# Second buffers for the loads of q and the split parts of k, later and earlier units for the loads of q, k and v, a shared ring of four tiles for five, and measured times in the scheduler of an attention and feed-forward kernel

## The chip, the core and the metric

The kernel runs on one core of a Trainium2 chip. The core has five engines that run their own instruction lists in order and wait for each other by semaphores: TensorE (PE in the profile, with weight loads as PEld), VectorE (DVE), ScalarE (ACT), GpSimd (POOL) and SyncE (SP). SP issues all DMAs of this kernel. The metric is the device time of one execution in microseconds, and shorter is better.

## What is computed

Attention over 8 batches of 8 heads with 1152 positions of 64 elements, where neighbouring pairs of queries are averaged first (576 queries a head), and then a feed-forward layer with the gate h * cos(h):

```python
def _attn_ref(q, k, v) -> np.ndarray:
    B, H, S, D = q.shape
    factor = 2
    scale = 1.0 / np.sqrt(D)
    q_pool = q.reshape(B, H, S // factor, factor, D).mean(axis=3)
    scores = scale * np.matmul(q_pool, k.transpose(0, 1, 3, 2))
    scores = scores - np.max(scores, axis=-1, keepdims=True)
    attn = np.exp(scores)
    attn = attn / (np.sum(attn, axis=-1, keepdims=True) + 1e-09)
    return np.matmul(attn, v).astype(np.float32)
...
def _moe_ref(x, w_in, w_out) -> np.ndarray:
    h = x @ w_in
    g = h * np.cos(h)
    return (g @ w_out).astype(np.float32)
```

All inputs are float32: q, k and v of 8 x 8 x 1152 x 64, `w_in` of 512 x 2048 and `w_out` of 2048 x 512. The 8 x 576 rows of the attention's result, with the heads side by side, are the 4608 rows of the feed-forward layer.

## The kernel before, in words

**Pairs and units.** The heads are taken two at a time: 32 pairs, four to a batch. A pair `p` has ten units. Unit 0 holds the 64 queries a head that are left over from 512, and units 1 to 9 hold one block of 128 keys each, for 512 queries of both heads. A unit is a matrix product of scores into the PSUM tile `st` (L860, or L880 for the leftover), the exponential on ACT (L901 or L906), and the product with v into `ava` and `avb` (L927), which is written one unit later.

**Split numbers.** Products are made in fp16 with each float32 operand split into a high part and a rest. For pairs 0 to 5 (`NDIR = 6`) the exponentials stay in float32 and L927 multiplies in float32. From pair 6 on the exponential is split: ACT copies the high part (L909), and POOL (L915) or, for every third unit, DVE (L911) subtracts it for the rest.

**Preparing q, k and v of a later pair.** Each pair needs, ahead of its units:

- k in two portions, J0 (four blocks) and J1 (five blocks): `load_k` (L556) into the tile `kld`, `prep_k` (ACT L584 makes the high part, POOL L585 the rest, both into `kst`), `transpose_k` (L630, a DMA transpose into `k1`), and `copy_k` (L637, DMAs into `k2`).
- q: `load_q` (four DMAs, two at L566 and two at L573, into `qld`), `pool_q` (POOL L591 adds neighbouring queries, in place in `qld`), `prep_q1` (ACT L602, from pair 6 on DVE L604: the high part into `q1s`), `transpose_q1` (L609), `prep_q2` (POOL L617 and L623: the rest from `qld` and `q1s` into `qs2`), and `transpose_q2` (L744). The last reader of a `qld` tile is `prep_q2`, so a `qld` buffer is free again after L623.
- row maxima of the scores: `mains`, `mx_rest` and others (PE L655, L673, L695, L712 into the PSUM tile `mx`, DVE L665, L683, L705, L722 reduce them), and `m_write` puts them into `qs2`.
- v: `load_v` (L750 into `vld`), `v_max_begin` (DVE L757, then L390 writes 128 single elements to the DRAM tile `row`, and L392 reads them back to all partitions as `am`), `v_max_end`, `prep_v` and `prep_v_lo`.

The table `JOBS` says in which unit of which pair each step of pair n is written: `(-2, 1, pool_q)` stands for unit 1 of pair n-2. `kld`, `kst`, `qld` and `vld` have one buffer each.

**The feed-forward stream.** `ffn1` (PE L1174, ACT L1198 and L1201, DVE L1202) and `ffn2` (PE L1234, DVE L1250) work on chunks of 256 rows; `ew_group` takes the cosine on ACT (L1110), multiplies on DVE (L1116) and splits the gate on ACT and POOL (L1127, L1128). A chunk can start when the four pairs of its batch are done and `w_in` is prepared, and `ffn2` when `w_out` is. While units are written, a credit of `FRATE` a unit sets how much of this stream is written between them; what is left after the last unit follows at the end. `weight_steps` (loads at L442, DVE L453 to L463, PE L471, ACT L493 and L494, POOL L495) prepares the weights; `SRATE` is how many of its steps are written in a unit, first until `w_in` is ready, then after. Raw weights, the float32 copies of `w_out`'s parts, and the tiles `hsc` and `y` of `ffn1` share one ring of `NBIG` tiles (`big_take`, `big_free`).

**What sets the order.** The program as written is not the order that runs. `arrange` takes all instructions, gives each a cost, and goes through time: of the instructions whose inputs are ready by its own clock, each engine takes the one that was written first. The five lists that come out are fixed with dependencies, and each engine then runs its list in order. The costs are formulas in `estimate` and `transfer`; PE's and SP's stand in `arrange` itself (lines 140 to 152). An instruction that waits on the chip holds up everything behind it in its engine's list.

Of the kernel before, what the change touches and what calls it, by code (L numbers as in the profile page):

```python
# [19 lines left out]
P = 128  # L20
# [7 lines left out]
NBIG = 5  # L28
# [12 lines left out]
SRATE = (1.0, 0.6)  # L41
# [8 lines left out]
    "vam": 4, "es": 1, "pps": 1, "amx": 4,  # L50
# [74 lines left out]
def arrange(tc, nc, extra):  # L125
# [3 lines left out]
    for i in rec:  # L129
        rd, wr = boxes(i)  # L130
        eng = str(i.engine).split(".")[-1]
        if eng == "PE":
# [9 lines left out]
            if rd[0][4] == 4:  # L142
                c = max(n_out(wr) * 0.00167 + 0.0025, 0.112)
# [4 lines left out]
        else:  # L148
            nd = dict(eng=eng, ins=[], rd=[], wr=[], cost=0.0, lock=False)
            nodes.append(nd)  # L150
            if eng == "SP":
                nd["cost"] = 0.06
                nd["dma"], nd["lat"] = transfer(type(i).__name__, rd[0], wr[0])
            else:
                nd["cost"], nd["lock"] = estimate(i, type(i).__name__, rd, wr)
                nd["func"] = str(getattr(i, "func", "")) if eng == "Activation" else ""
# [153 lines left out]
def tile_attention_ffn(  # L310
# [241 lines left out]
    def load_k(n, js):  # L552
        b, hp = divmod(n, HP)
        nj = js.stop - js.start
        kt = sb1.tile([P, 2, KT - RB, D], F32, tag="kld", name="kld")
        nc.sync.dma_start(  # L556
            kt[:, :, 0:nj],
            k[b, 2 * hp : 2 * hp + 2].rearrange("h (p j) d -> p h j d", p=P)[:, :, js],
        )
        kld[n] = kt[:, :, 0:nj]  # L560

    def load_q(n):
        b, hp = divmod(n, HP)
        qt = sb1.tile([P, NSL, 2, D], F32, tag="qld", name="qld")
# [14 lines left out]
    def prep_k(n, js):  # L579
        kv = kld[n].rearrange("p h j d -> p j h d")  # L580
        nj = js.stop - js.start
        ks = sb1.tile([P, KT - RB, 4, D], F16, tag="kst", name="kst")[:, 0:nj]
        hi = ks[:, :, 0::3, :]
        nc.scalar.copy(hi, kv)  # L584
        nc.gpsimd.tensor_sub(ks[:, :, 1:3, :], kv, hi)  # L585
        kst[n] = ks
# [42 lines left out]
    def transpose_k(n, js):  # L629
        nc.sync.dma_start_transpose(  # L630
            k1[n % 3][:, js].rearrange("p j h c -> p (j h) c"),
            kst.pop(n).rearrange("p j a d -> p (j a d)"),
# [168 lines left out]
    def mains(c, ts):  # L801
# [7 lines left out]
        (-2, 0, lambda n: load_k(n, J0)),  # L809
        (-2, 0, load_q),  # L810
# [3 lines left out]
        (-2, 2, lambda n: load_k(n, J1)),  # L814
# [9 lines left out]
        (-2, 7, prep_q2),  # L824
        (-2, 8, mains(1, (0,))),
        (-2, 8, load_v),
        (-2, 9, mains(1, (1,))),
        (-1, 0, lambda n: copy_k(n, J1)),
        (-1, 0, mains(1, (2,))),
        (-1, 0, v_max_begin),  # L830
# [6 lines left out]
        (-1, 4, v_max_end),  # L837
        (-1, 5, prep_v),
        (-1, 6, lambda n: prep_v_lo(n, (0,))),
        (-1, 7, lambda n: prep_v_lo(n, (1,))),  # L840
# [534 lines left out]
    for n in (0, 1):  # L1375
        for dp, di, fn in JOBS:
            if dp + n < 0:
                fn(n)
# [64 lines left out]
```

## Time and profile before

| what | value |
|---|---|
| median of 3 runs | 1691.94 us (1689.31 to 1700.04) |
| the profiled execution, its own time | 1687.24 us |
| its span, first to last instruction | 1685.5 us |
| mean granted TensorE clock | 0.971 |
| ACT busy | 1199.7 us (71%) |
| DVE busy | 1154.0 us (68%) |
| POOL busy | 877.0 us (52%) |
| DMA traffic | 147.28 MB, mean 87 GB/s |

The table is read from the left of the time: the span is the stretch that the profile explains, and the 1.7 us between it and the execution's own time lie around it. A share of busy time is a mean over stages that differ: at first there are only attention and weights, then attention and feed-forward together, and at the end the feed-forward stream alone. In a timeline row of the profile, the two numbers ahead of the engine are the start and the duration, and the bracket at the end is the idle time of that engine before the row, with what ended it.

### The profile page before, as it was taken

How to read it: one execution, taken by the hardware profiler on the slowest of the kernel's cores; microseconds unless marked ns; L12 is line 12 of the kernel's file. 1: busy time of each engine (PE TensorE's matmuls, PEld its weight loads, DVE VectorE, ACT ScalarE, POOL GpSimd, SP SyncE). 2: the span in 40 equal slices, each digit the busy share in tenths (PEclk: the TensorE clock that was granted, in tenths of full speed). 3: DMA queues.
4: the chain of work that ended last, by engine and by line, in shares of the span. 5: the costliest groups of instructions: out<-in, count | busy, mean ns of one | idle time of the engine just before them, and what ended most of it. 6: DMA issues, size and time to landing. Idle time of an engine off the chain costs nothing. (4 is left out here: it accounts for less than half of the span.)

```text
span 1685.5 us, 39430 instructions
## 1 busy us (share of the span) xinstructions
PE 1552.6 (92%) x16580; PEld 1058.8 (63%) x16580; DVE 1154.0 (68%) x1625; ACT 1199.7 (71%) x1468; POOL 877.0 (52%) x738
## 2 busy tenths in 40 slices
PE   2889799998999989988899999999999999998998
PEld 1667677765766566655666566666666657665664
DVE  6687878688767768866667676777768778642442
ACT  2465657788977777876787687987788878885542
POOL 3242334376465746556466465564757484653222
PEclk9799999999999999998999999999999999998999
DMA  9985852455336442434325424444434443011010
GB/s 206 197 187 130 181 128 34 90 83 129 54 78 108 83 88 56 108 61 96 72 64 99 90 57 91 89 71 96 105 70 88 94 86 80 17 35 26 13 32 19
DMA packets 340657, 147.28 MB, mean 87 GB/s; under 512 B 247808, under 2 KB 323584, under 8 KB 340480
## 3 DMA queue, kind: packets, MB, share of 16 engines
q1 hardware_dynamic: 340480, 144.78, 41.1%
q8 instruction: 129, 2.11, 0.6%
q14 instruction: 48, 0.39, 0.2%
HBM read 76.55 MB, written 10.50 MB: 52 GB/s over the span
## 5 line engine op out<-in xcount | busy, mean ns | idle before, releaser
L915 POOL TENSOR_TENSOR pp<-e,pp 128x512 f16<-128x512 f32 x348 | 424.9, 1243 | 289.6 <-ACT pp L909 182.6
L665 DVE TENSOR_REDUCE mxs<-mx 128x2 f32<-128x1024 f32 x252 | 307.7, 1221 | 135.7 <-PE mx L655 132.4
L1174 PE MATMUL f<-xT,w 128*128 128x256 f16 x3168 | 385.4, 276 | 10.5 <-DVE y L1202 6.4
L1174 PEld LDWEIGHTS <-w 128*128 128x128 f16 x3456 | 339.4, 99 | 84.3 <-issue 14.4
L906 ACT ACTIVATE e<-st,eb 128x1024 f32<-128x1024 f32 x260 | 288.8, 1111 | 139.6 <-PE st L860 113.4
L1234 PE MATMUL f<-w,g 128*128 128x512 f16 x1584 | 369.0, 382 | 0.0
L1234 PEld LDWEIGHTS <-g 128*128 128x128 f16 x1728 | 167.3, 99 | 193.7 <-issue 7.1
L909 ACT CAST pp<-e 128x1024 f16<-128x1024 f32 x260 | 271.4, 1044 | 10.9 <-PE ava L927 3.6
L927 PEld LDWEIGHTS <-pp 128*128 128x128 f16 (+1 forms) x6864 | 229.5, 100 | 66.8 <-POOL pp L915 19.0
L1128 POOL TENSOR_TENSOR g<-hsc,g 128x512 f16<-128x512 f32 x144 | 197.8, 1398 | 137.0 <-ACT g L1127 136.8
L927 PE MATMUL ava<-vc,pp 128*128 128x65 f16 (+4 forms) x4680 | 254.6, 205 | 13.7 <-POOL pp L915 11.4
L860 PE MATMUL st<-q1T,k 128*128 128x512 f16 x576 | 223.2, 388 | 21.0 <-ACT e L906 12.3
L860 PE MATMUL st<-q2T,k 128*128 128x512 f16 x576 | 223.6, 388 | 0.0
L927 PE MATMUL avb<-vc,pp 128*128 128x65 f16 (+2 forms) x3240 | 213.5, 205 | 5.5 <-POOL pp L915 5.5
L655 PE MATMUL mx<-k,q1T 128*128 128x512 f16 x504 | 154.3, 389 | 25.4 <-DVE mxs L665 14.4
L860 PEld LDWEIGHTS <-k 128*128 128x128 f16 x1152 | 104.1, 100 | 116.3 <-issue 32.4
L1116 DVE TENSOR_TENSOR hsc<-hsc,y 128x512 f32<-128x512 f32 x144 | 132.3, 964 | 36.2 <-ACT y L1110 35.9
L585 POOL TENSOR_TENSOR kst<-kld,kst 128x512 f16<-128x512 f32 x64 | 89.3, 1395 | 124.8 <-ACT kst L584 111.9
L1202 DVE SCALAR_TENSOR_TENSOR y<-f,r1a,y 128x512 f32<-128x512 f32 x132 | 98.2, 746 | 79.4 <-ACT y L1201 78.9
L911 DVE TENSOR_TENSOR pp<-e,pp 128x1024 f16<-128x1024 f32 x86 | 123.7, 1439 | 28.7 <-ACT pp L909 27.6
L1198 ACT ACTIVATE hsc<-f,r 128x512 f32<-128x512 f32 x132 | 90.0, 683 | 58.9 <-PE f L1174 58.3
L901 ACT ACTIVATE pp<-st,eb 128x1024 f32<-128x1024 f32 x60 | 66.7, 1112 | 79.1 <-PE st L860 66.0
(134 smaller groups left out, 1754.5 us busy)
## 6 DMA issues: line engine op xcount, KB each, us to landing
vld<-in_v_dram SPq DMA_DIRECT2D x32, 576.0 KB, 4.0
qld<-in_q_dram SPq DMA_DIRECT2D x64, 256.0 KB, 3.9
kld<-in_k_dram SPq DMA_DIRECT2D x32, 320.0 KB, 3.3
kld<-in_k_dram SPq DMA_DIRECT2D x32, 256.0 KB, 3.9
wraw<-in_moe_w_in_dram SPq DMA_DIRECT2D x8, 1024.0 KB, 7.4
wraw<-in_moe_w_out_dram SPq DMA_DIRECT2D x8, 1024.0 KB, 6.7
out_dram<-ob SPq DMA_DIRECT2D x32, 256.0 KB, 2.5
k<-k SPq DMA_DIRECT2D x64, 80.0 KB, 2.8
```

The lines of the kernel that those rows point to most:

```text
L655: nc.tensor.matmul(m[:, h, :], q1T[n][:, 2 * t + h, :], k1[n % 3][:, c * RB : (c + 1) * RB, h, :], start=True, stop=True, skip_group_check ...
L665: nc.vector.reduce_max(mxs[n][:, 2 * t : 2 * t + 2, c], m, axis=AX.X)
L860: nc.tensor.matmul(s[:, h, :].rearrange("p (t c) -> p t c", c=P), w[:, j, h, :], x[:, h : 2 * QT : 2, :], start=part == 0, stop=part == 1, ...
L906: nc.scalar.activation(e, s, AF.Exp, scale=exp_scale, bias=eb)
L909: nc.scalar.copy(pp[:, 0], e)
L911: nc.vector.tensor_sub(pp[:, 1], e, pp[:, 0])
L915: nc.gpsimd.tensor_sub(pp[:, 1, c], e[:, c], pp[:, 0, c])
L927: mm = nc.tensor.matmul(out, w, x, start=start, stop=False, skip_group_check=True)
L1116: nc.vector.tensor_mul(hj, hj, y[:, j : j + 2])
L1128: nc.gpsimd.tensor_sub(gt[:, 1], hj, gt[:, 0])
L1174: mm = nc.tensor.matmul(ps[:, fi, :], w1[wt][:, hp, fs], ck.xT[hp][:, xi, cs], start=n == 0, stop=n == 3 * HP - 1, skip_group_check=True,)
L1234: nc.tensor.matmul(po, gt[:, gi, f % 2, ts_], w2[wt][:, f, :], start=f == 0 and (gi, wt) == (0, 0), stop=f == NF - 1 and (gi, wt) == (1, 0),)
```

## The change

It has these parts:

- `qld` and `kst` get two buffers each, and `kld` and `kst` are remembered by pair and portion, so that two of them can be under way.
- `load_k` of J0 and `load_q` move from unit 0 of pair n-2 to units 5 and 6 of pair n-3. `load_k` of J1 moves from unit 2 to unit 1. `prep_q2` moves from unit 7 to unit 9, `load_v` from unit 8 of pair n-2 to unit 0 of pair n-1, and the steps on v behind it by one unit each. The steps written ahead of the first unit now include pair 2.
- `NBIG` goes from 5 to 4, and the first value of `SRATE` from 1.0 to 0.7.
- In `arrange`, the cost of a float32 matmul is doubled, and that of an SP instruction goes from 0.06 to 1.35 for a transpose and 0.55 for another DMA.

```diff
-NBIG = 5
+NBIG = 4
...
-SRATE = (1.0, 0.6)
+SRATE = (0.7, 0.6)
...
-    "vam": 4, "es": 1, "pps": 1, "amx": 4,
+    "vam": 4, "qld": 2, "kst": 2, "es": 1, "pps": 1, "amx": 4,
...
             if rd[0][4] == 4:
-                c = max(n_out(wr) * 0.00167 + 0.0025, 0.112)
+                c = 2 * max(n_out(wr) * 0.00167 + 0.0025, 0.112)
...
             if eng == "SP":
-                nd["cost"] = 0.06
+                nd["cost"] = 1.35 if "Transpose" in type(i).__name__ else 0.55
...
-        kld[n] = kt[:, :, 0:nj]
+        kld[n, js.start] = kt[:, :, 0:nj]
...
-        qt = sb1.tile([P, NSL, 2, D], F32, tag="qld", name="qld")
+        qt = sb1.tile([P, NSL, 2, D], F32, tag="qld", bufs=2, name="qld")
...
-        ks = sb1.tile([P, KT - RB, 4, D], F16, tag="kst", name="kst")[:, 0:nj]
+        ks = sb1.tile([P, KT - RB, 4, D], F16, tag="kst", bufs=2, name="kst")[:, 0:nj]
...
     JOBS = [
-        (-2, 0, lambda n: load_k(n, J0)),
-        (-2, 0, load_q),
+        (-3, 5, lambda n: load_k(n, J0)),
+        (-3, 6, load_q),
         (-2, 1, lambda n: prep_k(n, J0)),
         (-2, 1, pool_q),
         (-2, 1, lambda n: transpose_k(n, J0)),
-        (-2, 2, lambda n: load_k(n, J1)),
+        (-2, 1, lambda n: load_k(n, J1)),
...
-        (-2, 7, prep_q2),
         (-2, 8, mains(1, (0,))),
-        (-2, 8, load_v),
         (-2, 9, mains(1, (1,))),
+        (-2, 9, prep_q2),
         (-1, 0, lambda n: copy_k(n, J1)),
         (-1, 0, mains(1, (2,))),
-        (-1, 0, v_max_begin),
+        (-1, 0, load_v),
+        (-1, 1, v_max_begin),
...
-    for n in (0, 1):
+    for n in (0, 1, 2):
         for dp, di, fn in JOBS:
             if dp + n < 0:
                 fn(n)
```

No computation is added or left out. What moves is the order of nearly every list, and three places matter below. The numbers in the names count tiles in the order in which they are written, so one number is one pair's tile.

First SP, in the middle of the program, around the four loads of one q tile (`qld_6493` before, `qld_6847` now). Before:

```order
L566 DMA qld_6493<-in_q_dram 128x4x128
L573 DMA qld_6493<-in_q_dram 64x128 x2
L750 DMA vld_6333<-in_v_dram 128x2x576
L1081 DMA_TRANSPOSE xT_6371<-xs2_6245 128x8x128
L566 DMA qld_6493<-in_q_dram 128x4x128
L556 DMA kld_7179<-in_k_dram 128x2x256
L390 DMA row_6506<-mxa_6504 128x1
L637 DMA k2_0_69<-k1_0_105 64x5x128 x2
L630 DMA_TRANSPOSE k1_1_106<-kst_6750 128x10x128
L1081 DMA_TRANSPOSE xT_6872<-xs2_6738 128x8x128
L609 DMA_TRANSPOSE q1T_6682<-q1s_73 128x10x128
```

And now:

```order
L566 DMA qld_6847<-in_q_dram 128x4x128
L573 DMA qld_6847<-in_q_dram 64x128 x2
L390 DMA row_6478<-mxa_6476 128x1
L566 DMA qld_6847<-in_q_dram 128x4x128
L556 DMA kld_7211<-in_k_dram 128x2x320
L637 DMA k2_0_69<-k1_0_105 64x5x128 x2
L609 DMA_TRANSPOSE q1T_6568<-q1s_73 128x10x128
L630 DMA_TRANSPOSE k1_1_106<-kst_6649 128x10x128
```

Before, the transpose of q's high part that follows the loads (`q1T_6682`) is made from the tile just loaded; now it (`q1T_6568`) is made from the tile of the pair before, and that of `qld_6847` comes a pair later. Over all 32 pairs, the transpose that belongs to a q tile stands 3 to 8 rows of SP behind the tile's last load before, and 8 to 29 now. The write of `row` stands among these DMAs in both: up to eight rows ahead of the last load of a q tile for 18 pairs before, for 21 now.

Second POOL at the same place: L623 frees a q buffer, L591 works on a freshly loaded tile. Before, with one buffer, from the freeing of `qld_6493` to the next tile:

```order
L617 TENSOR_TENSOR qs2_71<-qld_6493,q1s_73 128x4x2x64
L623 TENSOR_TENSOR qs2_71<-qld_6493,q1s_73 64x64 x2
L585 TENSOR_TENSOR kst_7384<-kld_7323,kst_7384 128x5x128
L915 TENSOR_TENSOR pp_6989<-e_6987,pp_6989 128x512 x2
L915 TENSOR_TENSOR pp_7038<-e_7036,pp_7038 128x512 x2
L591 TENSOR_TENSOR qld_7181<-qld_7181 128x9x64
L915 TENSOR_TENSOR pp_7165<-e_7163,pp_7165 128x512 x2
```

And now, from the freeing of `qld_5343`, whose buffer `qld_6847` takes (`qld_6108` lies in the other):

```order
L617 TENSOR_TENSOR qs2_71<-qld_5343,q1s_73 128x4x2x64
L915 TENSOR_TENSOR pp_6096<-e_6094,pp_6096 128x512 x2
L623 TENSOR_TENSOR qs2_71<-qld_5343,q1s_73 64x64 x2
L585 TENSOR_TENSOR kst_7206<-kld_6782,kst_7206 128x4x128
L591 TENSOR_TENSOR qld_6847<-qld_6847 128x9x64
L915 TENSOR_TENSOR pp_6229<-e_6227,pp_6229 128x512 x2
L915 TENSOR_TENSOR pp_6283<-e_6281,pp_6283 128x512 x2
```

From pair 6 on, the median is three rows of POOL between the freeing of a buffer and L591 on the tile that takes it, before and now; what changed is that this tile is the one after the next.

Third DVE, where q's high part is made (L604) ahead of one pair, in the middle of the program. Before and now:

```order
L1202 SCALAR_TENSOR_TENSOR y_8389<-f_8687,r1a_91,y_8389 128x512
L604 CAST q1s_73<-qld_8670 128x1024
L665 TENSOR_REDUCE mxs_8252<-mx_8769 128x2
L604 CAST q1s_73<-qld_8670 64x128 x2
L397 TENSOR_REDUCE amx_8996<-am_8685 128x1
```

```order
L1202 SCALAR_TENSOR_TENSOR y_8434<-f_8598,r1a_91,y_8434 128x512
L604 CAST q1s_73<-qld_8352 128x1024
L604 CAST q1s_73<-qld_8352 64x128 x2
L397 TENSOR_REDUCE amx_9037<-am_8741 128x1
L401 TENSOR_SCALAR amx_9037<-amx_9037 128x1
```

The place of L604 among its neighbours is nearly the same; it reads a tile whose loads were issued one pair earlier than before. In PE's list the first row of L1174 stands behind the scores of 44 units' blocks before and of 53 now, that is about a pair later; from pair 16 on, the feed-forward rows stand between the same pairs' scores as before, and so does all that follows the last pair.

More of the change, by code (lines that the diff above doesn't have):

```diff
@@ L579, in prep_k @@
     def prep_k(n, js):
-        kv = kld[n].rearrange("p h j d -> p j h d")
+        kv = kld.pop((n, js.start)).rearrange("p h j d -> p j h d")
         nj = js.stop - js.start
-        ks = sb1.tile([P, KT - RB, 4, D], F16, tag="kst", name="kst")[:, 0:nj]
+        ks = sb1.tile([P, KT - RB, 4, D], F16, tag="kst", bufs=2, name="kst")[:, 0:nj]
         hi = ks[:, :, 0::3, :]
@@ L585, in prep_k @@
         nc.gpsimd.tensor_sub(ks[:, :, 1:3, :], kv, hi)
-        kst[n] = ks
+        kst[n, js.start] = ks
     def pool_q(n):
@@ L631, in transpose_k @@
             k1[n % 3][:, js].rearrange("p j h c -> p (j h) c"),
-            kst.pop(n).rearrange("p j a d -> p (j a d)"),
+            kst.pop((n, js.start)).rearrange("p j a d -> p (j a d)"),
         )
@@ L836, in tile_attention_ffn @@
         (-1, 4, transpose_q2),
[L837 to L840, printed above, removed]
+        (-1, 5, v_max_end),
+        (-1, 6, prep_v),
+        (-1, 7, lambda n: prep_v_lo(n, (0,))),
+        (-1, 8, lambda n: prep_v_lo(n, (1,))),
     ]
```

## The prediction

> **What bounds the kernel now.** I read the page first, then the waits of PE by releaser, then stretches of the time, and last the timelines of single stalls.
>
> ```profile
> span 1685.5 us, 39430 instructions
> PE 1552.6 (92%) x16580; PEld 1058.8 (63%) x16580; DVE 1154.0 (68%) x1625; ACT 1199.7 (71%) x1468; POOL 877.0 (52%) x738
> ...
> PEclk9799999999999999998999999999999999998999
> ```
>
> PE is busy for 92% of the span, and nothing else comes near. A change that adds and removes no product, like this one, can therefore only win what PE idles, and what PE loses while its clock is lowered behind an idle stretch. Where is that? The stages, with the granted clock in the third column from the right:
>
> ```profile
> core 0: us, PE busy (x) PEld busy (x) DVE busy (x) ACT busy (x) POOL busy (x), PEclk, DMA share, GB/s
> 0.00:60.00 60.00, 23.97 (x140) 11.56 (x140) 42.79 (x51) 15.73 (x21) 16.08 (x23) 0.88 0.91 190
> 60.00:300.00 240.00, 217.10 (x1839) 172.97 (x1839) 184.33 (x280) 144.73 (x176) 90.16 (x62) 0.96 0.64 143
> 300.00:1500.00 1200.00, 1136.85 (x13275) 763.11 (x13274) 861.84 (x1208) 949.80 (x1152) 713.41 (x610) 0.98 0.40 81
> 1500.00:1686.00 186.00, 174.72 (x1332) 111.11 (x1329) 65.04 (x89) 89.43 (x120) 57.35 (x46) 0.97 0.08 22
> ```
>
> PE idles 36.0 us in the head (60 - 23.97), 22.9 in the first pairs, 63.2 in the long middle and 11.3 at the end. In the middle the clock costs up to 1200 x (1 - 0.98) = 24 us more. The middle is what the second buffers aim at. Its idle time by releaser, and then single stretches of it:
>
> ```profile
> PE mx L880 <- DVE mxs L665: 15.2, 5, 6.9
> PE st L860 <- ACT e L906: 12.3, 10, 3.3
> PE ava L927 <- POOL pp L915: 10.3, 3, 4.2
> ...
> PE avb L927 <- POOL pp L915: 4.7, 4, 1.5
> ```
>
> ```profile
> 480.00:510.00 30.00, 26.33 (x305) 16.45 (x304) 20.30 (x27) 20.21 (x25) 14.82 (x13) 0.94 0.42 80
> 530.00:545.00 15.00, 12.27 (x117) 7.30 (x114) 6.99 (x13) 10.37 (x13) 5.89 (x6) 0.89 0.81 86
> ...
> 612.00:642.00 30.00, 22.45 (x251) 16.92 (x249) 16.86 (x23) 17.60 (x22) 7.61 (x6) 0.83 0.32 48
> ...
> 920.00:940.00 20.00, 15.87 (x156) 9.82 (x153) 8.32 (x10) 12.74 (x18) 8.62 (x8) 0.91 0.64 84
> 1040.00:1050.00 10.00, 6.66 (x87) 4.90 (x86) 4.03 (x10) 5.86 (x10) 5.04 (x5) 1.00 0.55 121
> ...
> 1215.00:1237.00 22.00, 19.74 (x243) 14.69 (x240) 12.91 (x16) 15.29 (x22) 10.15 (x10) 0.92 0.36 77
> 1250.00:1500.00 250.00, 248.29 (x2970) 169.44 (x2968) 180.77 (x263) 212.79 (x260) 153.93 (x134) 1.00 0.34 72
> ```
>
> The last row shows what the middle is without stalls: 1.7 us idle in 250 at full clock. The loss sits in twelve short stretches. In nine of them (the first here is 480:510, the largest 612:642, the last 1215:1237) POOL waits just ahead for a q load; they idle 41.9 us together. In three (530:545, 920:940, 1040:1050) ACT waits with L584 for the transpose that still reads the one `kst` buffer: 2.73 + 4.13 + 3.34 = 10.2 us. How a q load becomes a stall is seen at 612, on SP, POOL and DVE, and the `kst` wait at 930:
>
> ```profile
> 612.41 0.53 SPq L390 DMA_DIRECT2D row<-mxa  x1
> ...
> 613.55 1.15 SPq L566 DMA_DIRECT2D qld<-in_q_dram  x1
> ...
> 616.71 7.47 SPq L630 DMA_TRANSPOSE k<-kst  x1
> ...
> 625.09 1.40 POOL L591 TENSOR_TENSOR qld<-qld 128x576 f32<-128x576 f32 x1 [13.26 <-DMA qld<-in_q_dram]
> ...
> 626.52 1.62 DVE L604 CAST q1s<-qld 128x1024 f16<-128x1024 f32 x1 [9.13 <-POOL qld L591]
> ...
> 930.49 0.62 ACT L584 CAST kst<-kld 128x512 f16<-128x512 f32 x1 [7.17 <-DMA k<-kst]
> ```
>
> The second half of q is issued 1.1 us behind the write of `row`. It lands for POOL at 625.1, and the transpose issued next is held until 616.71 + 7.47 = 624.2, both some 12 us after the `row` write went out. POOL stands still for 13.3 us with its L915 rows behind L591, and DVE for 9.1 us with its reductions behind L604, because L604 needs that same q tile. So one late load reaches PE by two ways: by POOL (products wait for `pp`), and by DVE (which frees `mx` and `f`). In the middle, POOL is named for 10.3 + 4.7 = 15.0 us of PE's waits; I put all of these into the nine q stretches, which leaves 41.9 - 15.0 = 26.9 us that came by DVE or ACT.
>
> **The change, part by part.**
>
> *Second q buffer and earlier q load.* L604 now reads a tile that was loaded and added a pair earlier (the order of DVE and SP), so DVE no longer stands behind a fresh load. This row of DVE's waits goes, ten waits with it:
>
> ```profile
> DVE q1s L604 <- POOL qld L591: 48.7, 10, 9.3
> ```
>
> I take the 26.9 us as won whole; the ends are 0, if DVE finds another late wait in each place (it then waits for POOL's L623, which frees `q1s`), and 26.9. For POOL's own way I take nothing. A load can be issued when L623 has freed the buffer, and POOL's order still has a median of three rows between L623 and L591. The load's four issues, its landing and the `row` write stay between them, so POOL will go on waiting at L591 with L915 behind it; `prep_q2` two units later frees the buffer later too. The ends are -15.0 (all won) and +15.0 (as much again lost); the nearest row, the 13.3 us above, speaks for no change. The Trainium skill (DMA: Bandwidth & Descriptors, Queues, rings and completion order) says that each DMA engine consumes its descriptors in ring order, so a slow write holds what is issued behind it. By that page too POOL's part stays, and the 12 us above agree with it.
>
> *Second `kst` buffer.* ACT's L584 no longer waits for the transpose of the other portion. All of the 10.2 us go; ends 0 and 10.2. What is late next is ACT's wait for `kld`, whose J0 load now has six units' lead and whose J1 load has two instead of one.
>
> *The clock.* It is lowered behind stalls, which costs 24 us in the middle at most (above). I take it in proportion to the idle time that goes, 37.1 of 63.2 us: 14.1; ends 0 and 24. The Trainium skill (TensorE: Matmul & The Clock Gate, HAM oscillation) warns of gaps above about 3.4 us only. Here 530:545 is at 0.89 with 2.73 us idle in all, and 1040:1050 is at 1.00 with 3.34, so this trace does not bear the limit out. By the page, the 15 x 0.11 = 1.65 us of 530:545 would not be tied to its wait, the term would be 12.4, and the sum 1.7 us smaller.
>
> *The head.* PE's first product waits for q's transpose, and SP now issues four more DMAs ahead of it, the q loads of the next pair.
>
> ```profile
> 1.98 1.26 SPq L573 DMA_DIRECT2D qld<-in_q_dram  x2
> ...
> 3.91 0.58 SPq L566 DMA_DIRECT2D qld<-in_q_dram  x1
> ...
> 11.95 1.36 SPq L609 DMA_TRANSPOSE q1T<-q1s  x1
> ...
> 20.04 1.03 PE L655 MATMUL st<-k,q1T 128*128 128x512 f16 x2 [20.04 <-DMA q1T<-q1s]
> ```
>
> That is 2 x 0.58 + 1.26 = 2.4 us of issue and 576 KB, 3.0 us at the 190 GB/s of the first 60 us. Ends: 0, if they fit where SP waits, and 5.4; I take 4.
>
> *The first pairs.* `SRATE` 0.7 spreads the weight steps over more units, and the feed-forward stream starts a pair later. Two rows, pairs 1 to 3 without it and the next two with it:
>
> ```profile
> 92.80:208.80 116.00, 99.85 (x864) 77.17 (x864) 93.22 (x137) 67.22 (x82) 42.00 (x27) 0.99 0.73 162
> 208.80:312.20 103.40, 97.81 (x868) 78.39 (x867) 75.76 (x115) 69.37 (x84) 40.00 (x30) 1.00 0.41 85
> ```
>
> PE idles 13.9% without the stream (16.15 of 116) and 5.4% with it (5.59 of 103.4). Two more pairs of 38.7 us at the higher share cost 77 x 0.085 = +6.6; that is the upper end. The lower is -16, if the thinner weight work frees DVE (80% busy there) and the idle time of pairs 1 to 3 goes. I take +4. The products that start later are not lost: from pair 16 on the order has them beside the same pairs, and the end of the program is the same.
>
> *Costs in the scheduler.* The SP values fit the rows (1.36 a transpose, 0.58 a copy above). The doubled float32 cost, 224 ns, does not fit at full clock:
>
> ```profile
> 152.71 1.00 PE L927 MATMUL ava<-vc,pp 128*128 128x65 f32 x8
> ```
>
> Eight take 1.00 us, 125 ns each. It touches the order of pairs 0 to 5 alone, and lies in the ends of the term before.
>
> *The ring of four.* Nothing. `hsc` waits for products, not for a buffer: 58.3 of the 58.9 us of idle time before it.
>
> ```profile
> L1198 ACT ACTIVATE hsc<-f,r 128x512 f32<-128x512 f32 x132 | 90.0, 683 | 58.9 <-PE f L1174 58.3
> ```
>
> The rest, 0.6, is the trace's lower bound for a buffer; the upper is taken with the first pairs, where weights use the ring as well. *The v steps*: nothing either; each keeps its distance of units to the next, and `load_v` has one unit less ahead of it.
>
> *The sum*: -26.9 - 10.2 - 14.1 + 4 + 4 = -43.2. The profiled execution took 1687.24 us, so the sum gives 1644.0 there. The median of the runs is 4.7 us higher; I forecast 1691.9 - 43.2 = 1648.7, say 1649.
>
> **The rivals.**
>
> *All of it is won.* POOL's part goes too, with the whole clock: -26.9 - 15.0 - 10.2 - 24 + 4 + 4 = -68.1, 1624 us. For it: the q load can now be a pair early. Against it: the three rows of POOL between L623 and L591.
>
> *The change doesn't do what it says.* L604 waits for `prep_q2` on a POOL that still stands still, so DVE loses its time as before, and only `kst` is won: -10.2, a share of the clock (10.2 of 63.2, 3.9) and +8, that is -6, 1686 us. For it: POOL's order, and DVE's L604 has the same neighbours. Against it: L623 stands ahead of the waiting L591, not behind it.
>
> *Slower: q's transpose is held behind the `row` write.* `v_max_begin` moves to unit 1, so `row` is written one unit before `transpose_q1` instead of two, and SP's order has it a few rows ahead of L609 in most pairs. A hold of 12 us, as at 612, exceeds the two units until the first `mains`. A pair takes 47.4 us by this row ((1400.7 - 311.0) / 23), two units 9.5:
>
> ```profile
> L591 POOL TENSOR_TENSOR qld<-qld x24: 1395/1404/2397, 311.0 to 1400.7; 128x576 f32<-128x576 f32 x24
> ```
>
> PE would wait 2.5 us in each of 26 pairs: +65, 1714 us. From 43 / 26 = 1.7 us a pair it decides against the change. Against it: before, L609 stands behind `row` as well, and no PE wait for `q1T` is among the waits of the middle.
>
> **How the numbers follow.** Forecast (1630 to 1672): 0.55. All won (below 1630): 0.15. Only `kst` (1675 to 1709): 0.18. Slower: 0.12. A measurement of this kernel tells about 1% from no change, 17 us. So faster is 0.55 + 0.15 = 0.70, the same 0.18, slower 0.12. The range from 1618 to 1695 leaves out the slower case and some of the best and of the middle one, 0.2 together.
>
> **What would show it.** Right: the DVE row L604 <- POOL L591 is gone, ACT's waits for k's transposes are gone, POOL's waits for q loads remain, PE's idle time between 300 and 1500 is about half, and the clock there is at 0.99. The first product starts near 24 us. Wrong: PE waits for `q1T` in the middle, DVE waits for L623 by as much as for L591 before, or POOL's q waits are gone and PE's with them.

## The result, and the profile after

The changed kernel takes 1623.59 us (median of 4 runs, 1622.34 to 1629.64) beside 1695.22 us for the kernel before (4 runs, 1689.31 to 1700.04): a ratio of 0.959, with a 95% interval from 0.954 to 0.963. It is faster by 72 us, where 43 were forecast; the time is 25 us below the 1649, inside the range, but below the 1630 to 1672 of the prediction's own account, and it is that of the rival "all of it is won" (1624). The profiled execution took 1622.78 us against 1687.24, so 64.5 us have to be found in the two traces; the profiled execution of before was 8 us faster than the median of its runs.

First the page of the kernel after, its span, busy times and clock by fortieths:

```profile
span 1621.0 us, 39459 instructions
PE 1531.1 (94%) x16580; PEld 1050.2 (65%) x16580; DVE 1146.9 (71%) x1625; ACT 1197.8 (74%) x1468; POOL 877.5 (54%) x738
...
PEclk9999999999999999999999999999999999999999
```

PE has the same 16580 products and is busy for 21.5 us less, since its clock is lowered less (no 8 is left in the row). To see where the rest went, both spans are cut where the same work begins: at pair 0's first L860, at pair 6's, and at pair 31's. The windows of before, then of after; the columns are those of the prediction's windows (PE, PEld, DVE, ACT, POOL, clock, DMA share, GB/s):

```profile
0.00:43.50 43.50, 12.24 (x66) 5.18 (x67) 27.40 (x33) 9.61 (x14) 14.92 (x22) 0.91 0.92 209
43.50:312.20 268.70, 241.04 (x2026) 188.36 (x2025) 203.47 (x302) 159.90 (x193) 95.57 (x66) 0.96 0.64 140
312.20:1498.40 1186.20, 1123.05 (x13156) 753.33 (x13155) 857.98 (x1203) 939.36 (x1139) 707.55 (x605) 0.98 0.40 81
1498.40:1685.50 187.10, 176.32 (x1344) 111.89 (x1339) 65.13 (x89) 90.83 (x124) 58.95 (x47) 0.97 0.09 23
```

```profile
0.00:46.70 46.70, 16.63 (x71) 6.59 (x72) 25.77 (x32) 9.61 (x15) 15.72 (x23) 1.00 0.87 201
46.70:274.90 228.20, 207.43 (x1808) 162.70 (x1807) 191.66 (x284) 130.12 (x156) 77.32 (x55) 0.96 0.84 170
274.90:1432.70 1157.80, 1130.53 (x13369) 769.08 (x13368) 865.22 (x1222) 967.81 (x1176) 725.48 (x614) 0.99 0.41 82
1432.70:1621.00 188.30, 176.54 (x1345) 111.81 (x1341) 64.29 (x89) 90.30 (x123) 58.99 (x47) 0.98 0.09 23
```

Read as they stand, pairs 0 to 5 won 40.5 us and the middle 28.4. But work moved between the two. The windows of the lines L1174 and L1234 alone in pairs 0 to 5 (PE and PEld), L1174 of before, L1234 of before, L1174 of after, and then the two kinds in the chain of after, where nothing stands between them:

```profile
43.50:312.20 268.70, 33.46 (x288) 28.09 (x288) 0.96 0.64 140
43.50:312.20 268.70, 4.05 (x18) 1.76 (x18) 0.96 0.64 140
```

```profile
46.70:274.90 228.20, 11.13 (x96) 9.43 (x96) 0.96 0.84 170
```

```profile
1017.26 2.62 PE f L1174 x24
1029.34 3.88 PE f L1234 x18
```

L1234 has no row in pairs 0 to 5 of after. So 288 - 96 = 192 products at 2.62 / 24 = 0.109 us and 18 at 3.88 / 18 = 0.216 went to the middle: 20.9 + 3.9 = 24.8 us of work. Net of it, by stage:

| stage | before | after | difference | net of moved work | predicted |
|---|---|---|---|---|---|
| head | 43.5 | 46.7 | +3.2 | +3.2 | +4 |
| pairs 0 to 5 | 268.7 | 228.2 | -40.5 | -15.7 | +4 |
| pairs 6 to 30 | 1186.2 | 1157.8 | -28.4 | -53.2 | -51.2 |
| pair 31 and the rest | 187.1 | 188.3 | +1.2 | +1.2 | 0 |

The middle came out near its sum, and the first pairs did not. In the middle PE's idle time fell from 63.2 to 27.3 us, 35.9 of the 53.2; the other 17.3 is time in which PE was busy at a lower clock. (The two digits of the clock allow a loss of 18 to 30 us before and 6 to 17 now.) What PE waits for there now, and what POOL waits for on q in the same stage, before and after (total, times, longest):

```profile
PE st L860 <- ACT e L906: 10.3, 8, 3.9
PE st L880 <- ACT e L906: 3.6, 1, 3.6
PE mx L695 <- DVE mxs L683: 3.1, 2, 2.2
PE avb L927 <- POOL pp L915: 0.8, 1, 0.8
PE ava L927 <- POOL pp L915: 0.8, 1, 0.8
PE mx L880 <- DVE mxs L665: 0.2, 1, 0.2
```

```profile
POOL qld L591 <- DMA qld<-in_q_dram: 72.4, 12, 13.3
```

```profile
POOL qld L591 <- DMA qld<-in_q_dram: 34.4, 8, 8.8
```

POOL still stands 34.4 us for q loads, but PE's waits for POOL fell from 15.0 to 1.6, and its largest wait of before, `mx` of L880 for DVE (15.2), is down to 0.2. The reason for the second is DVE: L604's row for POOL's L591 (48.7 us before) is gone from the waits of the whole run. What is left for it is a wait for `prep_q2` (L617), which frees `q1s`:

```profile
DVE q1s L604 <- POOL qs L617: 1.3, 2, 0.8
```

One place shows it whole. At 1150 of after, from the timelines of SP and POOL, and the window of the place:

```profile
1154.60 0.41 SPq L390 DMA_DIRECT2D row<-mxa  x1
1155.06 0.59 SPq L566 DMA_DIRECT2D qld<-in_q_dram  x1
...
1160.65 4.16 SPq L609 DMA_TRANSPOSE q1T<-q1s  x1
```

```profile
1165.10 1.41 POOL L591 TENSOR_TENSOR qld<-qld 128x576 f32<-128x576 f32 x1 [8.77 <-DMA qld<-in_q_dram]
```

```profile
1150.00:1170.00 20.00, 19.90 (x270) 15.75 (x268) 13.61 (x15) 14.28 (x20) 10.91 (x10) 1.00 0.70 102
```

The q load behind the write of `row` is late as it was at 612 before (10.5 us from the write to L591, 12.7 there), the transpose is held as well (4.16 us, 7.47 there), and POOL waits 8.8 us. PE is busy for 19.90 of the 20 us. At this place the chip still does what made the stall, and PE no longer depends on it.

### The profile page after: what moved, and what is told of

The parts are those of the page before. It is cut to its first block, busy times and chain, and to the rows that moved or that the text cites. A ratio compares the mean times of both kernels' runs of the same rounds, so it can differ in the third digit from the quotient of the medians.

```text
span 1621.0 us, 39459 instructions
## 1 busy us (share of the span) xinstructions
PE 1531.1 (94%) x16580; PEld 1050.2 (65%) x16580; DVE 1146.9 (71%) x1625; ACT 1197.8 (74%) x1468; POOL 877.5 (54%) x738
## 4 chain that ended last, share of the span: by engine, by line
PE 79%; DMA 6%; DVE 6%; ACT 5%; SPq 2%; issue 2%; POOL 1%; ACTq 0%; DVEq 0%; POOLq 0%
PE f L1234 21%; PE f L1174 18%; PE st L860 13%; PE ava L927 7%; PE avb L927 6%; PE mx L655 5%; DMA kld<-in_k_dram 2%; DVE mxs L665 2%; PE mx L695 2%; ACT e L906 1%; PE st L880 1%; PE mx L1234 1%; DMA am<-row 1%; DMA row<-mxa 1%; PE avb L1174 1%
## 5 line engine op out<-in xcount | busy, mean ns | idle before, releaser
L1174 PEld LDWEIGHTS <-w 128*128 128x128 f16 x3456 | 337.9, 99 | 77.7 <-issue 8.8
L1174 PE MATMUL f<-xT,w 128*128 128x256 f16 x3168 | 380.6, 274 | 7.1 <-DMA xT<-xs 4.6
L1234 PE MATMUL f<-w,g 128*128 128x512 f16 x1584 | 363.5, 379 | 0.0
L1234 PEld LDWEIGHTS <-g 128*128 128x128 f16 x1728 | 166.1, 98 | 190.9
L927 PE MATMUL ava<-vc,pp 128*128 128x65 f16 (+4 forms) x4680 | 250.9, 203 | 3.6 <-POOL pp L915 1.9
L860 PE MATMUL st<-q1T,k 128*128 128x512 f16 x576 | 220.7, 383 | 14.5 <-ACT e L906 10.3
L860 PE MATMUL st<-q2T,k 128*128 128x512 f16 x576 | 220.3, 382 | 0.0
L1116 DVE TENSOR_TENSOR hsc<-hsc,y 128x512 f32<-128x512 f32 x144 | 135.6, 988 | 51.8 <-ACT y L1110 51.7
L860 PEld LDWEIGHTS <-k 128*128 128x128 f16 x1152 | 102.4, 99 | 105.9 <-issue 22.0
L585 POOL TENSOR_TENSOR kst<-kld,kst 128x512 f16<-128x512 f32 x64 | 93.6, 1462 | 110.3 <-ACT kst L584 104.8
```

Source lines behind the costliest of these rows:

```text
L860: nc.tensor.matmul(s[:, h, :].rearrange("p (t c) -> p t c", c=P), w[:, j, h, :], x[:, h : 2 * QT : 2, :], start=part == 0, stop=part == 1, ...
L927: mm = nc.tensor.matmul(out, w, x, start=start, stop=False, skip_group_check=True)
L1116: nc.vector.tensor_mul(hj, hj, y[:, j : j + 2])
L1174: mm = nc.tensor.matmul(ps[:, fi, :], w1[wt][:, hp, fs], ck.xT[hp][:, xi, cs], start=n == 0, stop=n == 3 * HP - 1, skip_group_check=True,)
L1234: nc.tensor.matmul(po, gt[:, gi, f % 2, ts_], w2[wt][:, f, :], start=f == 0 and (gi, wt) == (0, 0), stop=f == NF - 1 and (gi, wt) == (1, 0),)
```

## The experiments

Twelve kernels ran. The table has them all, with the ratio to the kernel before in runs of the same chip, the stages net of feed-forward work, and what the theories differ on: PE's idle time in the middle, L604's waits for POOL, and the transposes on SP that took over 2.5 us to issue (their number and sum). In the kernels with one q buffer (before, e1, e3, e7, e10) all of L604's wait is for the fresh tile of L591; in those with two, none is, and all of it is for `prep_q2` (L617, L623). The stages and waits are of one profiled execution each.

| kernel | median us | ratio [95%] | pairs 0 to 5, net | middle, net | idle in middle | L604 for POOL | slow transposes |
|---|---|---|---|---|---|---|---|
| before | 1695.2 | | 233.4 | 627.5 | 63.2 | 48.7 | 15, 69.6 |
| after | 1623.6 | 0.959 [0.954, 0.963] | 217.8 | 574.4 | 27.3 | 1.3 | 15, 69.4 |
| e1 | 1676.7 | 0.987 [0.982, 0.993] | 238.8 | 619.0 | 58.7 | 48.6 | 12, 49.4 |
| e2 | 1657.1 | 0.978 [0.974, 0.982] | 240.7 | 586.7 | 34.8 | 15.5 | 17, 78.7 |
| e3 | 1681.9 | 0.992 [0.989, 0.995] | 244.7 | 617.1 | 57.5 | 45.8 | 17, 67.9 |
| e4 | 1619.3 | 0.955 [0.951, 0.959] | 229.0 | 563.2 | 21.6 | 0 | 15, 70.7 |
| e5 | 1631.0 | 0.963 [0.958, 0.968] | 239.6 | 570.3 | 24.2 | 3.4 | 15, 68.6 |
| e6 | 1636.1 | 0.965 [0.961, 0.970] | 225.1 | 579.7 | 33.9 | 1.3 | 16, 79.6 |
| e7 | 1649.6 | 0.973 [0.969, 0.978] | 261.4 | 565.1 | 15.5 | 4.7 | 2, 6.6 |
| e8 | 1585.8 | 0.935 [0.931, 0.940] | 204.1 | 559.4 | 12.6 | 2.4 | 9, 29.3 |
| e9 | 1634.1 | 0.965 [0.960, 0.969] | 230.1 | 572.1 | 21.0 | 2.2 | 15, 58.5 |
| e10 | 1607.7 | 0.949 [0.944, 0.955] | 221.2 | 568.5 | 20.9 | 2.3 | 5, 16.5 |
| e11 | 1663.1 | 0.982 [0.977, 0.987] | 249.0 | 586.9 | 36.5 | 12.7 | 15, 63.7 |
| e12 | 1646.9 | 0.970 [0.963, 0.976] | 228.1 | 589.4 | 38.8 | 10.7 | 17, 59.9 |

**e1: the scheduler's costs alone**, on the kernel before.

```diff
-                c = max(n_out(wr) * 0.00167 + 0.0025, 0.112)
+                c = 2 * max(n_out(wr) * 0.00167 + 0.0025, 0.112)
...
-                nd["cost"] = 0.06
+                nd["cost"] = 1.35 if "Transpose" in type(i).__name__ else 0.55
```

> The kernel before with the new costs in the scheduler alone (float32 matmul doubled, SP 1.35 and 0.55); buffers, units, SRATE and the ring as before. If the buffers make the gain of the middle and the costs at most that of the first pairs (my theory): 1675 to 1695 us, DVE waits for L591 in the middle stay at 30 to 50 us. If the costs in the scheduler make the gain, through a truer order (rival): 1640 to 1655 us, and those waits go although q has one buffer.

Measured: 1676.7, within the expected times, about 20 us faster than its runs of before (1696.5). The waits of L604 are untouched (48.6), so this gain is not the buffers'. It is a gain of the order alone. Where it lies is not shown: the profiled execution is the slowest of the four (1682.80) and its span is only 4.5 us below that of before.

**e2: all but these costs and `SRATE`**, on the kernel after.

```diff
-SRATE = (0.7, 0.6)
+SRATE = (1.0, 0.6)
...
-                c = 2 * max(n_out(wr) * 0.00167 + 0.0025, 0.112)
+                c = max(n_out(wr) * 0.00167 + 0.0025, 0.112)
...
-                nd["cost"] = 1.35 if "Transpose" in type(i).__name__ else 0.55
+                nd["cost"] = 0.06
```

> The changed kernel with the costs and SRATE of before: second buffers, new units and the ring of four remain. By my theory the middle keeps its gain of some 53 us and the first pairs lose theirs of some 16: 1635 to 1650 us. By the rival (the costs make the gain) 1675 us or more.

Measured: 1657.1, 39 us faster than before, and 7 us slower than the expected times: the middle keeps 40.8 of its 53 us, and the first pairs are 7 us longer than before. PE still waits 12.6 us for POOL in the middle, and L604 15.5 us for `prep_q2`. PE's largest wait for POOL there:

```profile
PE ava L927 <- POOL pp L915: 11.0, 6, 5.7
```

With e1's 20 us that makes 59 of the 72; `SRATE`, which is in neither, is worth 7 by e5, and the 6 that are left are within the spread of the runs.

**e3: one q buffer again**, with `load_q` and `prep_q2` at their old units, the rest as after.

```diff
-    "vam": 4, "qld": 2, "kst": 2, "es": 1, "pps": 1, "amx": 4,
+    "vam": 4, "kst": 2, "es": 1, "pps": 1, "amx": 4,
...
-        (-3, 6, load_q),
+        (-2, 0, load_q),
...
+        (-2, 7, prep_q2),
         (-2, 8, mains(1, (0,))),
...
-        (-2, 9, prep_q2),
```

> The changed kernel with one q buffer; load_q and prep_q2 stand in the units of before (unit 0 and unit 7), since with one buffer the load can't be written ahead of prep_q2. By my theory the q stalls come back: 1655 to 1670 us, DVE waits for L591 of 30 us or more in the middle. If q's second buffer does little, because POOL waits at L591 either way (rival): 1620 to 1635 us.

Measured: 1681.9, 58 us slower than after and 12 us above the expected times. By stages it is 42.7 us slower in the middle and 26.9 in the first pairs. PE's idle time in the middle is back (57.5), and so is the wait that the second buffer is there for. Among DVE's waits of e3 (total, times, longest):

```profile
DVE q1s L604 <- POOL qld L591: 45.8, 12, 6.2
```

This is the largest part of the change, and in the middle the mechanism is the forecast one.

**e4: one `kst` buffer again**, the rest as after.

```diff
-    "vam": 4, "qld": 2, "kst": 2, "es": 1, "pps": 1, "amx": 4,
+    "vam": 4, "qld": 2, "es": 1, "pps": 1, "amx": 4,
...
-        ks = sb1.tile([P, KT - RB, 4, D], F16, tag="kst", bufs=2, name="kst")[:, 0:nj]
+        ks = sb1.tile([P, KT - RB, 4, D], F16, tag="kst", name="kst")[:, 0:nj]
```

> The changed kernel with one kst buffer. By my theory 10 us of idle time and some 4 of clock come back: 1634 to 1642 us, ACT waits for k's transposes near 20 us. If the transposes are no longer held, since the q load stands elsewhere (rival), the second kst buffer has nothing left to do: 1620 to 1630 us.

Measured: 1619.3, just below the rival's range, and the intervals of the two ratios overlap; the second `kst` buffer brings nothing that can be measured. From the views of the tile `kst`, what its writers waited for on transposes (total, times), in before, in after and in e4:

```profile
  DMA k<-kst: 20.7, 8
```

```profile
  DMA k<-kst: 2.4, 2
```

```profile
  DMA k<-kst: 9.2, 3
```

More than half of these waits goes with one buffer too; in e1, with no second buffer at all, 3.3 us are left. They fall with the order of k's steps, and the 9.2 that stay cost no time: PE's idle time in the middle is 21.6, less than in after.

**e5, e6, e12: one number undone each**, on the kernel after: `SRATE` back to 1.0, the float32 cost back to 0.112, SP's cost back to 0.06.

```diff
-SRATE = (0.7, 0.6)
+SRATE = (1.0, 0.6)
```

> The changed kernel with the first SRATE back at 1.0. If the gain of the first pairs (some 16 us, feed-forward work counted out) comes from the weight steps being thinner: 1632 to 1642 us, all of the difference ahead of pair 6. If it comes from the order that the costs or the q buffer make: 1617 to 1629 us.

```diff
-                c = 2 * max(n_out(wr) * 0.00167 + 0.0025, 0.112)
+                c = max(n_out(wr) * 0.00167 + 0.0025, 0.112)
```

> The changed kernel with the float32 matmul's cost back at 0.112, which is what eight of them in a row take at full clock. If the doubled cost helps the first pairs although it is wrong: 1632 to 1642 us, all of the difference ahead of pair 6. If it does nothing: 1617 to 1629 us. If the true cost is better: below 1617 us.

```diff
-                nd["cost"] = 1.35 if "Transpose" in type(i).__name__ else 0.55
+                nd["cost"] = 0.06
```

> The changed kernel with SP's cost in the scheduler back at 0.06. e2 undid SRATE and both costs and lost 33 us to the changed kernel; e5 and e6 lost 7 and 12 with one of them each. If the parts add up, SP's cost is worth the remaining 14: 1632 to 1642 us. If only the float32 cost and SRATE matter, and e2's rest is chance of the order: 1618 to 1629 us.

Measured: 1631.0, 1636.1 and 1646.9, that is 7, 12.5 and 23 us slower than after. e5 lies between its two expected ranges, e6 in the first of its own but with only a part of the difference ahead of pair 6, and e12 above its own. e5's window of the first pairs, and that of pairs 1 to 3 in it, show where `SRATE` acts:

```profile
46.50:311.00 264.50, 230.56 (x1944) 182.82 (x1944) 202.82 (x300) 150.61 (x180) 90.67 (x62) 0.94 0.75 147
```

```profile
83.10:213.00 129.90, 108.12 (x863) 85.19 (x862) 103.83 (x151) 69.20 (x83) 48.25 (x30) 0.91 0.78 154
```

Net of feed-forward work this is 239.6 us beside 217.8 in after: more than what the first pairs had won is gone. Pairs 1 to 3 take 129.9 us, 108.4 in after, and that is nearly the whole difference. This profiled execution is the slowest of e5's four, 1639.23 us, 16.5 more than that of after; the medians differ by 7 only, so the 21.8 of this stage are an upper bound for what `SRATE` does in most runs. The SP cost works in the middle (589.4 beside 574.4): POOL's waits for q loads rise to 97.0 us in the whole run, from 72.0 in after, L604's for `prep_q2` to 10.7 from 1.3, and PE's for POOL in the middle to 7.7 from 1.6.

```profile
POOL qld L591 <- DMA qld<-in_q_dram: 97.0, 23, 12.1
```

The float32 cost, 224 ns where in the trace of before the 16 products from 152.71 on start 112 ns apart, helps all the same. (The prediction's 125 ns for one of eight counts in the end of the last.) Why it helps is not settled: the effect spreads over the first pairs (+7.3 when undone) and the middle (+5.3), and no single wait carries it.

**e11: the second q buffer alone**, on the kernel before, with the units of `load_q` and `prep_q2`, the pairs written ahead, and the ring of four.

```diff
-NBIG = 5
+NBIG = 4
...
-    "vam": 4, "es": 1, "pps": 1, "amx": 4,
+    "vam": 4, "es": 1, "pps": 1, "amx": 4, "qld": 2,
...
-        (-2, 0, load_q),
+        (-3, 6, load_q),
...
-        (-2, 7, prep_q2),
...
+        (-2, 9, prep_q2),
...
-    for n in (0, 1):
+    for n in (0, 1, 2):
```

> The kernel before with the second q buffer, load_q and prep_q2 in their new units, pair 2's load ahead of the first unit, and the ring of four; nothing else of the change. By my prediction's terms the middle wins 26.9 us of idle time and a share of the clock, POOL's part staying: 1650 to 1665 us, DVE waits for L591 below 10 us in the middle, PE waits for POOL there 10 us or more. If POOL's part goes too: 1640 us or less. If costs and the other units are needed for it: 1675 us or more.

Measured: 1663.1, 33 us faster than before, the greater part of e2's 39, and within the expected times. L604's wait for L591 is gone whole. Here the wait that was named as the other end of this step does appear, as in e2: L604 waits for POOL's `prep_q2`, which frees `q1s` (12.7 us, with the 1.9 for L623). PE waits 8.0 us for POOL in the middle, where 10 or more were expected. From the waits of DVE, and of PE in the middle:

```profile
DVE q1s L604 <- POOL qs L617: 10.8, 3, 7.9
```

```profile
PE ava L927 <- POOL pp L915: 7.5, 1, 7.5
```

So the buffer alone takes the long wait away and leaves a shorter new one, of which 1.3 us are left in the whole change.

**e7 and e8: no write of `row`.** The other theory is that the second q buffer only covers what the write of `row` does on SP's queue. Both kernels replace the write and the read by one float32 product with an identity `eye`, which POOL makes once at the start, and a reduction on DVE, e7 on the kernel before (with `NBIG` 4), e8 on the kernel after. The maxima are the same ones.

```diff
-        row = dram.tile([1, P], F32, tag=tag, bufs=4, name="row")
-        nc.sync.dma_start(row.rearrange("a p -> p a"), mx)
-        am = sb2.tile([P, P], F32, tag="es", name="am", bufs=1)
-        nc.sync.dma_start(am, row.broadcast_to([P, P]))
+        ps = psum.tile([P, P], F32, tag="f", bufs=2, name="vmp")
+        nc.tensor.matmul(
+            ps, mx.broadcast_to([P, P]), eye, start=True, stop=True, skip_group_check=True
+        )
+        am = sb2.tile([P, 1], F32, tag="amx", bufs=4, name="amx")
+        nc.vector.reduce_max(am, ps, axis=AX.X)
         return am
```

> The kernel before (with a ring of four tiles, to make room), where the maximum of v over partitions is taken by one float32 product with the identity and a reduction, instead of the write of row and its reading back; 64 small DMAs fewer. If the write of row is what holds the q loads behind it (theory): DVE waits for L591's line in the middle fall from 49 to below 15 us and the time is 1645 to 1668 us, with one q buffer. If the load's own four issues and its landing are too long for the three rows of POOL (rival): those waits stay above 35 us and the time is 1680 us or more.

> The changed kernel with the same replacement of row. If row holds the DMAs behind it: POOL's waits for q loads fall from 72 to below 30 us, DMA transposes whose issue takes over 2.5 us fall from 15 to below 5, and the time is 1600 to 1616 us. If the traffic of q, k and v itself holds them: waits above 55 us, as many long issues, 1617 to 1630 us.

Measured: e7 takes 1649.6, 47 us less than before with one q buffer, as expected; e8 takes 1585.8, 38 us less than after and 14 us less than the fastest expected. In e7 the slow transposes are nearly gone (2 beside 15), L604 waits 4.7 us, and PE's idle time in the middle is 15.5, less than in the kernel after; its first pairs are 28 us longer than before, so the middle alone won 62. In e8 two of the expected signs did not come: POOL still waits 47.0 us for q loads (7.5 in the middle, 34.4 in after), and 9 slow transposes are left, where below 30 us and below 5 were expected. So the write is not the only thing that holds a transpose. The window of e7 in the middle, and e8's first pairs and middle:

```profile
300.00:1400.00 1100.00, 1084.24 (x12738) 736.59 (x12738) 833.45 (x1167) 917.92 (x1117) 681.99 (x590) 1.00 0.40 87
```

```profile
41.00:255.60 214.60, 206.75 (x1820) 164.19 (x1819) 185.78 (x277) 129.56 (x155) 81.97 (x58) 0.97 0.76 178
255.60:1398.30 1142.70, 1130.15 (x13417) 772.60 (x13414) 859.04 (x1222) 967.91 (x1176) 712.06 (x611) 1.00 0.39 81
```

e8 beats both kernels: 0.935 of before [0.931, 0.940].

**e9: the write alone put back**, on e8, read by nothing.

```diff
         nc.vector.reduce_max(am, ps, axis=AX.X)
+        row = dram.tile([1, P], F32, tag=tag, bufs=4, name="row")
+        nc.sync.dma_start(row.rearrange("a p -> p a"), mx)
         return am
```

> The changed kernel with the maximum of v taken by the product, as in e8, and the write of row left in, read by nobody. If the write itself holds the DMAs behind it (theory): DMA transposes whose issue takes over 2.5 us rise from 9 to 14 or more, PE's idle time between pairs 6 and 31 from 13 to 20 us or more, and the time is 1605 to 1625 us. If e8 won by the shorter path of v and the missing read of row alone (rival): 1584 to 1595 us, and the issues stay as in e8.

Measured: 1634.1, 48 us slower than e8, and slower than the expected time. There are 15 slow transposes again and 21.0 us of idle time in the middle, as the theory of the write expected, but only 6 of the 15 were issued within 10 us behind a write. Of the 46 us between the two profiled executions, 12.7 lie in the middle, 26.0 in the first pairs and 6.5 in the head. The hold is seen on SP's timeline of e9 (its lines are shifted by the edit: L396 is the write, L575 the q load, L618 and L639 the transposes of q and k, L646 k's copies, L1265 the output):

```profile
990.41 0.34 SPq L396 DMA_DIRECT2D row<-mxa  x1
991.01 1.17 SPq L1265 DMA_DIRECT2D out_dram<-ob  x2
992.23 0.60 SPq L575 DMA_DIRECT2D qld<-in_q_dram  x1
993.96 1.35 SPq L646 DMA_DIRECT2D k<-k  x2
995.40 5.27 SPq L618 DMA_TRANSPOSE q1T<-q1s  x1
1000.72 1.32 SPq L639 DMA_TRANSPOSE k<-kst  x1
```

The transpose, issued in 1.32 us when nothing holds it (the last row), ends at 1000.67, 10.3 us behind the write. No engine waits for this write, so its price is the hold on the queue and what the order made of one DMA more. e9 is 10 us slower than the kernel after, which has the read as well; the intervals of the two ratios overlap, and in the traces the difference lies in the first pairs (+12.3), while the middle is 2.3 us shorter. The part of the order in the 48 us can't be told from the part of the hold by this run.

**e10: no write of `row`, and one q buffer**, e8 with the edit of e3.

> e8 with one q buffer, load_q and prep_q2 in the units of before. If the second q buffer is a remedy for loads that land late behind row, it has little left to do in the middle: that stretch, feed-forward work counted out, stays within 10 us of e8's 559, and the time is 1585 to 1605 us. If the second buffer is worth its 58 us (e3 against the changed kernel) by itself: 1630 us or more.

Measured: 1607.7, 22 us slower than e8 and a little above the expected time. With the write in place the second buffer is worth 58 us (e3), without it 22, and of these only 9.1 lie in the middle (568.5 beside 559.4, where e3 has 42.7); the rest lies in the first pairs. So in the middle the buffer is for the most part a remedy for the write.

## Why the prediction was right, and where it was not

**The second q buffer, by way of DVE: right.** The wait of 48.7 us is gone, undoing the buffer costs 58 us (e3), and alone it gives 33 (e11). The rival "the change doesn't do what it says" is out by the same rows: L604 does wait for `prep_q2`, for 12.7 us in e11 and 15.5 in e2, but far less than the 48.7 it was to replace.

**POOL's own part: mis-sized.** It was taken as 0, with -15.0 as one end; it came out at -13.4 (15.0 to 1.6). For the buffer the reason given for 0 holds: with the buffers and units alone (e2) PE still waits 12.6 us for POOL in the middle. The rest of the change takes these waits away: they are 7.7 without SP's cost (e12), 5.6 without `SRATE` (e5) and 2.6 without the float32 cost (e6). The costs alone do not do it either (e1, 17.1). The prediction gave none of the three an effect here. POOL's waits for q loads, which were to remain, fell by half (72.4 to 34.4), and what is left seldom reaches PE: at 1150 POOL waits 8.8 us and PE has work all the while. Which work moved there was not isolated.

**The sum of the middle: close, in part by luck.** PE's idle time there fell by 35.9 us, where 37.1 were forecast, but not by the same waits. By the rows of its waits, those for DVE fell from 28.5 to 8.3, for ACT from 18.8 to 14.3, for POOL from 15.0 to 1.6, and 2.7 that have no releaser are new. So DVE and ACT gave 24.7 of the 26.9 + 10.2 that were taken for them, and POOL's 13.4, taken at nothing, made up for the rest.

**The second `kst` buffer: the waits went, but not by the buffer.** ACT's waits for k's transposes went (20.7 to 2.4), but more than half of them go without the buffer (e4), and nearly all with the costs alone (e1, 3.3 left). So they belong to the order of k's steps and of SP; what they cost PE was not measured by itself.

**The clock: 14.1 forecast, 17.3 left over** after the idle time in the middle. It followed the idle time, somewhat more than in proportion.

**The head: right**, +4 forecast and +3.2 measured. The first product waits until 23.7 (before 20.0, forecast "near 24"):

```profile
PE st L655 <- DMA q1T<-q1s: 23.7, 1, 23.7
```

**The first pairs: the step that failed.** +4 was taken between the ends -16 and +6.6; -15.7 was measured. The 19.7 us between them are nearly all of the 21.3 by which the profiled execution won more than the 43.2 of the sum. The step was added up from pairs 1 to 5 alone and left pair 0 as it was. Pair 0 of before (its pairs 1 to 3 and 4 to 5 are in the prediction), then pair 0, pairs 1 to 3 and pairs 4 to 5 of after, and pair 0 of e3:

```profile
43.50:92.80 49.30, 43.38 (x295) 32.80 (x294) 34.49 (x52) 23.31 (x28) 13.57 (x10) 0.80 0.93 204
```

```profile
46.70:82.70 36.00, 33.35 (x284) 24.86 (x283) 33.18 (x43) 19.11 (x23) 8.74 (x7) 1.00 1.13 242
82.70:191.10 108.40, 99.45 (x862) 78.00 (x861) 92.92 (x144) 67.49 (x83) 43.63 (x31) 0.95 0.78 161
191.10:274.90 83.80, 74.63 (x666) 59.85 (x664) 65.56 (x98) 43.51 (x51) 24.94 (x19) 0.96 0.78 149
```

```profile
41.60:89.60 48.00, 43.24 (x295) 32.84 (x294) 36.41 (x49) 20.59 (x25) 11.54 (x9) 0.79 0.81 190
```

Pair 0 won 13.3 us, 10 of them as busy time at a clock of 1.00 instead of 0.80. Pairs 1 to 3 won 7.6, about half of what the lower end allowed (16.1 us idle before, 9.0 now). Pairs 4 and 5, net of the moved 24.8, lost 5.2, near the upper end's 6.6. Pair 0's gain comes with the second q buffer and its earlier loads: e3 loses 12.0 of it again, and pair 0 takes 46 to 53 us in the five kernels with one q buffer and 34 to 42 in the nine with two. Why the clock stays up there was not isolated. `SRATE` acts in pairs 1 to 3 (e5), where DVE works 92.9 us in after and 103.8 in e5; that it frees an engine, as the lower end supposed, fits this. Every part that was undone lengthens the whole stage, by 7 to 27 us (e6 7.3, e12 10.3, e4 11.2, e5 21.8, e3 26.9), so these prices can't be added.

**The scheduler's costs: too small.** The float32 cost was placed in pairs 0 to 5 alone, and SP's cost got no term at all. Alone they are worth 20 us (e1), and SP's cost has most of its effect in the middle: undone, 15.0 us there and 10.3 in the first pairs (e12).

**All of it is won: the same number by coincidence.** That rival's 1624 has -76.1 in the middle, where -53.2 were measured, and +4 in the first pairs, where it was -15.7.

**Slower, by q's transpose behind `row`: did not come.** SP holds some of them as that rival said: 6 transposes of q's high part behind the write took 4.16 to 7.59 us. PE waits for `q1T` nowhere in the middle; how much margin was left there was not measured.

**The ring of four and the v steps** were costed at nothing. No run undid them one by one, so this was not tested. A price of the ring in the first pairs is not excluded: the four kernels with the ring of four and `SRATE` at 1.0 take 239.6 to 261.4 us there (e5, e2, e11, e7), and before takes 233.4.

The cases' prices add up in no simple way: undone one at a time, the q buffer, SP's cost, the float32 cost and `SRATE` are worth 58 + 23 + 12.5 + 7 = 100 us, and the whole change is worth 72. Each part also decides how late the others may be.

## What to carry to other kernels

When a late transfer stalls the bound engine by several engines, follow each way apart and ask which engine stands still only because its instruction reads the fresh tile; a second buffer there can free the bound engine although the transfer is as late as ever. Then ask why the transfer is late: here a write of 512 bytes in single elements on the same queue was a main cause, and removing it with its reading back gained 47 us where the buffer around it gained 33, and both, with the rest of the change, 110 (e8). When a stage's term is added up from some of its pairs, look at the others too: most of the miss here lay in the one pair that no row was read for. In a kernel whose order a scheduler makes, its costs are a part of the change like any other; price them by a run of their own, since 20 us can come from the order alone.

## What the runs showed of the hardware

The write of 128 single elements is slow to land, and what SP issues right behind it lands late too. From the DMA view of after (KB each, median us from issue to landing), a load of q and the write:

```profile
qld<-in_q_dram SPq DMA_DIRECT2D x64, 256.0 KB, 3.6
```

```profile
row<-mxa SPq DMA_DIRECT2D x32, 0.5 KB, 8.6
```

The trace knows few landings: 4 writes in after, 7.7 to 9.4 us, and 23 in all kernels that have them, 6.9 to 10.9. The 7 DMAs of after that were issued within 3 us behind a write, and whose landing is known, took 6.8 to 10.6 us; those further than 12 us behind one have a median of 3.2. The same hold is seen in 10.5 us from the write to L591 at 1154.60 of after, and 10.3 to the end of the transpose in e9. A transpose takes about 1.35 us to issue; of the 15 in after and the 15 in e9 that took over 2.5 us, 10 and 6 were issued within 10 us behind a write. Another 24 and 22 issued as close behind one took less, and e8 without any write has 9 over 2.5 us, up to 5.0, so the write is not the only condition. Put back with no reader it cost 48 us, 1.5 us for each of its 32 writes, with an unknown share of the order. The packets of e8 and e9 show what it is made of, in the views of DMA:

```profile
DMA packets 331441, 145.17 MB, mean 92 GB/s; under 512 B 242688, under 2 KB 314368, under 8 KB 331264
```

```profile
DMA packets 336050, 145.20 MB, mean 89 GB/s; under 512 B 247296, under 2 KB 318976, under 8 KB 335872
```

e9 has 247296 - 242688 = 4608 packets under 512 bytes more, 144 for each of 32 writes: the 128 elements and 16 others. The Trainium skill (DMA: Bandwidth & Descriptors, Why a DMA increments its semaphore by 16 and not by 1) says that one descriptor moves one contiguous run, and that each of up to 16 engines ends its part with a write to the semaphore; the 128 and the 16 agree with it. The same page (Specifications) says that transfers below 512 bytes are done by reading, changing and writing back; whether that is what makes these writes slow, no run here shows.
